# An attention-and-MLP kernel: later additions of narrow inputs, another bank, 1e-9 on VectorE and matmuls of 128 columns

## The chip, the cores and the metric

The kernel runs on one core of a Trainium2 chip. The metric is device time in microseconds (us), the median of some runs. The core has TensorE (PE in the profile; PEld is its loading of weights), VectorE (DVE), ScalarE (ACT), GpSimd (POOL) and SyncE (SP), which here starts all transfers between memories. Each engine takes its own instructions in order and waits on semaphores for the others.

## What is computed

Attention with a local causal softmax and a linear memory branch, gated per head, and behind it two MLPs in a row:

```python
scores = np.matmul(q, k.transpose(0, 1, 3, 2)) / sqrt(D)     # B, H, S, D = 4, 8, 576, 64; causal
a = exp(scores - max); a /= a.sum(-1) + 1e-09
local = a @ v
q_p = elu(q) + 1
mem_out = (q_p @ M_prev) / (q_p . z_prev + 1e-6)
x = g * mem_out + (1 - g) * local                             # g = sigmoid(beta), per head
x = elu(x.reshape(2304, 512) @ w_in) @ w_out                  # 512 -> 2048 -> 512
out = leaky(x @ w_in2, 0.01) @ w_out2
```

The weights of the MLPs come as 64-bit floats and are decoded on the chip.

## The kernel before

**Numbers as two parts.** Most matmuls work on fp32r, a 32-bit form whose products are less exact than fp32's. A number is kept as a high part (rounded to fp32r) and a low part (the rest), and a product is two or three matmuls. In batch 0 of attention the tensors are plain fp32 instead (`full_v`); the trace shows such a matmul as two records.

**Attention.** A `Pair` is two heads of one batch, 16 pairs in all; an `Item` is one head and one of two groups of queries (the first 256 tokens, the last 320), 64 in all. Tokens are cut into five chunks `CH`, of 128, 128, 64, 128 and 128. An item goes through three stages, woven so that item n is scored while item n-1 is transposed and item n-2 multiplied with v: `score` (matmuls of a chunk of queries with all earlier keys into a bank `sc`, of which there are three; DVE adds the mask and finds the extreme; ACT takes the exponential and its sum `ss`), `norm` (1e-9 is added to the sums on GpSimd, DVE takes the reciprocal `rs`, GpSimd scales the probabilities `pt`), `t0` to `t1c` (transposes into two `tp` banks, split into high `dh`, `ah` and low `dl`, `al` by ACT and DVE) and `pv` (the product with v and, in the same sum, of the memory branch's queries `qph`, `qpl` with M, into one bank `po`; batch 0 uses `pm`). `qp_unit` transposes those queries, in the same bank `po`, ahead of a pair's first `pv`. DVE copies the result to `xp` (L529), SP writes it to memory as `xq`, one tensor for each head of a pair and batch.

**Where half is zeros.** Chunk 0 has 128 keys, but its score matmul is made 256 wide (L414). The diagonal blocks of the probabilities stand in `dh`, `dl` or `d32` as four pieces of 128 columns; the first piece is zeros, set once, so that `vc[j, 1]` and `vc[j, 4]` can be multiplied with 256 columns, zeros and diagonal (L510, L518).

**The first MLP's first part, woven in.** `phase1_units(ti)` makes the work of one batch for seven of sixteen slices of 128 hidden numbers, as two parts of 288 tokens each. A part is `u_x` (SP loads x, as `xt` and, with the halves of the partitions exchanged, `x2`, tile `y`; DVE adds the two, four instructions, L684; ACT casts to `xh`, GpSimd takes the rest `xl`, and both go to memory), seven `u_h` (12 matmuls into `pm`, L616, then elu: ACT, ACT, DVE to `e`, L630, split into `gh` and `gl`) and four `u_o` (21 matmuls, L644). The tiles `x` and `y` exist once. Batch 0 is read from `xm` without an addition.

**What sets the order.** The loop over attention units emits this work as fill: from `DELAY` = 13000 (ns of planned PE work) behind the end of a batch, against a credit in proportion to the attention emitted, with a priority 20 instructions ahead. What is left goes into `side`, behind attention, together with the decoding of more weights. A scheduler then orders each engine's instructions by these priorities and a timing model of its own; the order that it made is what runs. Banks: `pm` 2, `sc` 3, `tp` 2, `po` 1.

Of the kernel before, what the change touches and what calls it, by code (L numbers as in the profile page):

```python
# [8 lines left out]
F32 = mybir.dt.float32  # L9
# [3 lines left out]
ALU = mybir.AluOpType  # L13
AX = mybir.AxisListType

P = 128
# [3 lines left out]
def _f(ap):  # L20
    return ap.bitcast(F32)
# [3 lines left out]
def kernel(  # L25
# [14 lines left out]
    nc = tc.nc  # L40
# [4 lines left out]
    NKC = DM // P  # L45
    NF = DFF // P
    NFA = 7
# [4 lines left out]
    V32 = 1  # L52
# [3 lines left out]
    HC = 1.0  # L56
    E_GH, E_WH, E_VH, E_MS, E_V32, E_XH, E_RS, E_Y = "V", "A", "V", "P", "P", "A", "P", "A"
    W2A, W2B = 1, 5
# [7 lines left out]
    EARLY = 150  # L66
    DELAY = 13000.0
    NHP = H // 2
    PSUM = bass.MemoryType.PSUM
# [134 lines left out]
    def bank(tag):  # L204
        return psum.tile([P, 512], F32, tag=tag, bufs=BANKS[tag], name=tag)
# [44 lines left out]
    class Pair:  # L250
# [69 lines left out]
        def qp_unit(self, grp):  # L320
            _, s0, n, cc = grp
            if grp is self.groups[0]:
                self.qph = at.tile([P, S], F32R, tag="qph", name="qph")
                self.qpl = at.tile([P, S], F32R, tag="qpl", name="qpl")
            tp = bank("po" if self.ti else "pm")
            for c in cc:
# [73 lines left out]
    class Item:  # L400
# [8 lines left out]
        def score(self, c):  # L409
# [3 lines left out]
            qs, kk, kl = pr.qs[j], pr.kk[0 if pr.full_v else j], pr.pad["kl", j]  # L413
            spans = [(0, nk, max(nk, 256))] if c < 4 else [(0, 288, 288), (288, 288, 288)]  # L414
            if c == 2:
# [82 lines left out]
        def pv(self):  # L498
# [8 lines left out]
            if gi == 0:  # L507
                for a in ("d32",) if full else ("dh", "dl"):
                    mms.append((0, n, pr.vc[j, 0], pd[a][:, 256:512]))
                    mms.append((0, n, pr.vc[j, 1], pd[a][:, 0:256]))  # L510
            else:
# [4 lines left out]
                for a in ("d32",) if full else ("dh", "dl"):  # L516
                    mms.append((64, n, pr.vc[j, 3], pd[a][:, 256:512]))
                    mms.append((64, n, pr.vc[j, 4], pd[a][:, 0:256]))  # L518
            if full:
# [138 lines left out]
    def phase1_units(ti):  # L658

        units = []  # L660
        for pi, (pt, o, w, _) in enumerate(parts):
            if pt != ti:
                continue
            st = {}

            def u_x(pi=pi, o=o, w=w, st=st):
                def split():
                    st["x"] = split_x(xt, w, pi % 2)
                    for n in range(2):
                        nc.sync.dma_start(xp_scr[n][pi], _f(st["x"][n]))  # L670
                    st["g"] = {}

                xt = mtile("x", 1, F32, (NKC, NW))[:, :, 0:w]
                if ti < V32:
                    nc.sync.dma_start(xt, xm_scr[ti][:, :, o:o + w])
                    split()
                    return
                x2 = mtile("y", 1, F32, (NKC, NW))[:, :, 0:w]
                for j in range(2):
                    ps, pz = slice(64 * j, 64 * j + 64), slice(64 - 64 * j, 128 - 64 * j)  # L680
                    nc.sync.dma_start(xt[ps], xq_scr[ti][j][ps, :, o:o + w])
                    nc.sync.dma_start(x2[ps], xq_scr[ti][j][pz, :, o:o + w])
                for c in range(NKC):
                    nc.vector.tensor_tensor(out=xt[:, c], in0=xt[:, c], in1=x2[:, c], op=ALU.add)  # L684
                split()

# [11 lines left out]

            units.append((0, u_x))
            for f in range(NFA):  # L700
                units.append((HC * 12 * w / 2.4, lambda f=f, u=u_h: u(f)))
            for ec in range(NKC):
                units.append((3 * NFA * w / 2.4, lambda ec=ec, u=u_o: u(ec)))
        return units

# [47 lines left out]
    for c, u, done in att:  # L753
# [7 lines left out]
        if done is not None:  # L761
            fill += [(pos + DELAY, c2, u2) for c2, u2 in phase1_units(done)]
        if fill and fill[0][0] <= pos:
# [164 lines left out]
```

## Time and profile before

| | us |
|---|---|
| median of 3 runs | 1096.52 (1096.45 to 1099.43) |
| the profiled execution | 1098.26 |
| its span, first to last instruction | 1096.2 |
| PE busy | 1057.6 |
| DVE busy | 600.3 |
| POOL busy | 530.6 |
| ACT busy | 484.8 |
| mean granted PE clock | 0.995 of full speed |

By the last P·V matmul of each batch, attention on batch 0 ends at 99.9 us, and batches 1, 2 and 3 end at 198.0, 306.2 and 404.1; the rest is MLP. Matmuls overlap and their ends are modelled, so a busy PE may still lose time between starts; how long a matmul holds PE is read from the distance of its start to the next start. Durations on POOL are rough. A wait is put down to the semaphore that came last by the profile.

### The profile page before, as it was taken

What the parts mean: (1) busy time and instruction counts of PE and PEld (TensorE: products, weight loads), DVE (VectorE), ACT (ScalarE), POOL (GpSimd) and SP (SyncE); (2) the same over time, 40 slices, a digit from 0 to 9 for tenths busy, and PEclk for the clock granted to TensorE, in tenths of its full rate; (3) what the DMA queues carried; (4) which work ended last, traced back from release to release, by engine and by line L of the source; (5) the groups of instructions that cost most, each with busy time, mean ns of one, the idle gap of its engine ahead of it and who ended that gap; (6) DMA issues with size and microseconds to landing.
All of it is one profiled execution on the core that took longest, in us unless ns stands there. A gap on an engine that the chain in (4) does not pass through costs nothing.

```text
span 1096.2 us, 17406 instructions
## 1 busy us (share of the span) xinstructions
PE 1057.6 (96%) x5904; PEld 912.7 (83%) x5904; DVE 600.3 (55%) x1398; ACT 484.8 (44%) x1169; POOL 530.6 (48%) x674
## 2 busy tenths in 40 slices
PE   6998899989998999999999999999999999999997
PEld 3777789979998999978877889888888888888896
DVE  6889987778878857566574314664321222232232
ACT  5988877777877645444343223432211110111110
POOL 7675675667667626455453224755422322222221
PEclk9999999999999999999999999999999999999999
DMA  7753643564365139665653304331200100010010
GB/s 181 189 144 91 188 115 99 124 169 145 78 178 156 59 81 271 225 215 185 219 189 119 98 18 116 135 116 39 77 1 1 58 20 1 1 39 1 1 39 20
DMA packets 151576, 115.05 MB, mean 105 GB/s; under 512 B 81728, under 2 KB 144192, under 8 KB 151488
## 3 DMA queue, kind: packets, MB, share of 16 engines
q1 hardware_dynamic: 151488, 113.95, 35.5%
q8 instruction: 47, 0.77, 0.3%
q14 instruction: 41, 0.34, 0.1%
HBM read 78.52 MB, written 31.85 MB: 101 GB/s over the span
## 4 chain that ended last, share of the span: by engine, by line
PE 73%; DMA 8%; DVE 7%; POOL 3%; ACT 3%; SPq 3%; issue 3%; DVEq 0%; POOLq 0%; ACTq 0%
PE pm L616 17%; PE sc L876 14%; PE tp L616 13%; PE sc L644 8%; PE po L876 4%; PE pm L644 4%; PE po L522 3%; PE tp L455 3%; PE po L644 2%; DMA wraw<-in_moe_w_out_dram 2%; DMA x<-xq 2%; SPq L212 2%; PE sc L426 1%; PE sc L427 1%; PE pm L522 1%
## 5 line engine op out<-in xcount | busy, mean ns | idle before, releaser
L623 POOL TENSOR_TENSOR gl<-e,gh 128x512 fp32r<-128x512 f32 (+2 forms) x181 | 199.8, 1108 | 369.8 <-DVE gh L241 291.9
L616 PE MATMUL tp<-xw,w 128*128 128x512 f32 (+1 forms) x504 | 145.4, 371 | 0.9 <-DVE e L630 0.9
L616 PE MATMUL pm<-xw,w 128*128 128x512 f32 (+1 forms) x496 | 143.9, 371 | 0.0
L876 PE MATMUL sc<-w,gh 128*128 128x512 f32 x448 | 137.7, 393 | 0.0
L449 POOL TENSOR_SCALAR pt<-pt,rs,omg 128x128 f32<-128x128 f32 (+4 forms) x160 | 102.7, 651 | 28.0 <-DVE rs L444 25.7
L616 PEld LDWEIGHTS tp<-xw,w 128*128 128x128 f32 x504 | 91.3, 188 | 19.7 <-DVE e L630 1.7
L644 PE MATMUL sc<-gh,w 128*128 128x512 f32 (+2 forms) x438 | 106.0, 343 | 1.1 <-DVE st L857 0.7
L616 PEld LDWEIGHTS pm<-xw,w 128*128 128x128 f32 x496 | 90.5, 188 | 18.5
L434 ACT ACTIVATE pt<-pt,mx 128x128 f32<-128x128 f32 (+4 forms) x160 | 93.2, 585 | 22.7 <-DVE mx L429 22.1
L876 PEld LDWEIGHTS sc<-w,gh 128*128 128x128 f32 x448 | 83.1, 188 | 17.9
L616 PE MATMUL tp<-xv,w 128*128 128x512 f32 (+1 forms) x252 | 93.2, 370 | 0.0
L616 PE MATMUL pm<-xv,w 128*128 128x512 f32 (+1 forms) x248 | 92.0, 371 | 0.0
L616 PE MATMUL pm<-xh,w 128*128 128x288 f32 x368 | 80.2, 305 | 9.1 <-DVE e L630 5.7
L635 ACT ACTIVATE e<-pm 128x512 f32<-128x512 f32 (+1 forms) x40 | 22.2, 556 | 150.3 <-PE pm L616 149.1
L455 PE MATMUL tp<-ident,pt 128*128 128x128 f32 x480 | 80.1, 276 | 8.0 <-DVE al L248 3.1
L241 DVE CAST gh<-e 128x512 fp32r<-128x512 f32 (+2 forms) x146 | 77.9, 537 | 16.9 <-PE po L644 4.2
L137 POOL TENSOR_TENSOR w<-wm,w 128x512 fp32r<-128x512 f32 x50 | 66.1, 1344 | 43.4 <-ACT w L239 43.4
L876 PE MATMUL sc<-w,gl 128*128 128x512 f32 x224 | 85.4, 393 | 0.0
L644 PEld LDWEIGHTS sc<-gh,w 128*128 128x128 f32 x438 | 74.6, 188 | 12.2 <-issue 1.5
L636 DVE TENSOR_TENSOR e<-tp,e 128x512 f32<-128x512 f32 (+1 forms) x40 | 25.5, 637 | 107.2 <-ACT e L635 107.1
L636 DVE TENSOR_TENSOR e<-pm,e 128x512 f32<-128x512 f32 (+1 forms) x40 | 25.5, 637 | 105.8 <-ACT e L635 105.8
L429 DVE CUSTOM_DVE_ANT_0 pt<-sc,mask 128x128 f32<-128x128 f32 (+4 forms) x160 | 69.4, 446 | 8.6 <-PE sc L427 4.3
(155 smaller groups left out, 2407.9 us busy)
## 6 DMA issues: line engine op xcount, KB each, us to landing
wraw<-in_moe_w_in_dram SPq DMA_DIRECT2D x32, 512.0 KB, 4.1
wraw<-in_moe_w_out_dram SPq DMA_DIRECT2D x32, 512.0 KB, 5.3
xh<-xh SPq DMA_DIRECT2D x8, 576.0 KB, 3.3
xl<-xl SPq DMA_DIRECT2D x8, 576.0 KB, 3.9
ys<-st SPq DMA_DIRECT2D x32, 144.0 KB, 3.0
x1s<-st SPq DMA_DIRECT2D x36, 128.0 KB, 1.9
x<-x1s SPq DMA_DIRECT2D x9, 512.0 KB, 3.9
out_dram<-st SPq DMA_DIRECT2D x36, 128.0 KB, 1.7
```

The costliest lines, as they stand in the source:

```text
L137: nc.gpsimd.tensor_tensor(out=w[:, 1, a], in0=t[:, a], in1=_f(w)[:, 0, a], op=ALU.subtract)
L241: (nc.vector if eng == "V" else nc.gpsimd).tensor_copy(dst, src)
L429: nc.vector.tensor_tensor_reduce(out=pt[0:m, k0:k0 + n], in0=sc[0:m, 0:n], in1=mk, op0=ALU.add, op1=ALU.min, scale=-0.125, scalar=mx[0:m, ...
L434: nc.scalar.activation(out=pt[0:m, 0:nk], in_=pt[0:m, 0:nk], func=AF.Exp, scale=-1.0, bias=mx[0:m, last:last + 1], accum_out=self.pd["ss"] ...
L449: nc.gpsimd.tensor_scalar(out=pt, in0=pt, scalar1=rs[0:m, i:i + 1], scalar2=omg[0:m, h:h + 1], op0=ALU.mult, op1=ALU.mult,)
L455: nc.tensor.transpose(dst, self.p[c][:, k0:k0 + kn], ident)
L522: nc.tensor.matmul(po[:, a:b], w, x, start=i == 0, stop=i == len(mms) - 1)
L616: nc.tensor.matmul(ph, wi[:, wj, kc, :], xx[:, kc, :], start=n_mm == 0, stop=n_mm == 11)
L623: nc.gpsimd.tensor_tensor(out=gl, in0=g, in1=_f(gh), op=ALU.subtract)
L636: nc.vector.tensor_tensor(out=t, in0=ph, in1=t, op=ALU.max)
L644: nc.tensor.matmul(py, wo[:, wj, ec * P:(ec + 1) * P], gg, start=opens and f == first and n_mm == 0, stop=closes and f == last and n_mm == 2,)
L876: nc.tensor.matmul(pos[tb], gg[:, tb * P:(tb + 1) * P], wo[:, wj, :], start=f == 0 and n_mm == 0, stop=f == NF - 1 and n_mm == 2,)
```

## The change

- `phase1_units` is cut anew. Loads of x become a unit of their own, `u_load`. Those of a batch's first part are emitted as soon as the batch is done; those of the second part after the first part's second `u_h`, and its additions and casts (`u_x`) after the sixth, where they stood ahead of its own first `u_h`. The fill of batches 1 to 3 starts `LATE` = 20000 behind the batch's end.
- `qp_unit` takes its bank from `sc` instead of `po`, except in batch 0.
- 1e-9 is added on DVE (`E_RS`).
- The score matmul of chunk 0 is 128 wide; the products with `vc[j, 1]` and `vc[j, 4]` are 128 wide, on the diagonal block alone.

```diff
-    E_GH, E_WH, E_VH, E_MS, E_V32, E_XH, E_RS, E_Y = "V", "A", "V", "P", "P", "A", "P", "A"
+    E_GH, E_WH, E_VH, E_MS, E_V32, E_XH, E_RS, E_Y = "V", "A", "V", "P", "P", "A", "V", "A"
+    LATE = 20000.0
...
-            tp = bank("po" if self.ti else "pm")
+            tp = bank("sc" if self.ti else "pm")
...
-            spans = [(0, nk, max(nk, 256))] if c < 4 else [(0, 288, 288), (288, 288, 288)]
+            spans = [(0, nk, nk)] if c < 4 else [(0, 288, 288), (288, 288, 288)]
...
-                    mms.append((0, n, pr.vc[j, 1], pd[a][:, 0:256]))
+                    mms.append((128, n, pr.vc[j, 1], pd[a][:, 128:256]))
...
-                    mms.append((64, n, pr.vc[j, 4], pd[a][:, 0:256]))
+                    mms.append((192, n, pr.vc[j, 4], pd[a][:, 128:256]))
...
+        mine = [(pi, o, w, {}) for pi, (pt, o, w, _) in enumerate(parts) if pt == ti]
+
+        def u_load(pi, o, w, st):
+            xt = st["t"] = mtile("x", 1, F32, (NKC, NW))[:, :, 0:w]
+            if ti < V32:
+                nc.sync.dma_start(xt, xm_scr[ti][:, :, o:o + w])
+                return
+            x2 = st["t2"] = mtile("y", 1, F32, (NKC, NW))[:, :, 0:w]
+            for j in range(2):
+                ps, pz = slice(64 * j, 64 * j + 64), slice(64 - 64 * j, 128 - 64 * j)
+                nc.sync.dma_start(xt[ps], xq_scr[ti][j][ps, :, o:o + w])
+                nc.sync.dma_start(x2[ps], xq_scr[ti][j][pz, :, o:o + w])
+
+        def u_x(pi, o, w, st):
+            xt = st["t"]
+            if ti >= V32:
                 for c in range(NKC):
-                    nc.vector.tensor_tensor(out=xt[:, c], in0=xt[:, c], in1=x2[:, c], op=ALU.add)
-                split()
+                    nc.vector.tensor_tensor(out=xt[:, c], in0=xt[:, c], in1=st["t2"][:, c], op=ALU.add)
+            st["x"] = split_x(xt, w, pi % 2)
...
+        units = [(0, lambda: u_x(*mine[0]))]
+        for k, (pi, o, w, st) in enumerate(mine):
...
             for f in range(NFA):
                 units.append((HC * 12 * w / 2.4, lambda f=f, u=u_h: u(f)))
+                if k + 1 < len(mine) and f == 1:
+                    units.append((0, lambda k=k: u_load(*mine[k + 1])))
+                if k + 1 < len(mine) and f == NFA - 2:
+                    units.append((0, lambda k=k: u_x(*mine[k + 1])))
...
-        return units
+        return lambda: u_load(*mine[0]), units
...
-            fill += [(pos + DELAY, c2, u2) for c2, u2 in phase1_units(done)]
+            fetch, more = phase1_units(done)
+            fetch()
+            start = pos + (DELAY if done < V32 else LATE)
+            fill += [(start, c2, u2) for c2, u2 in more]
```

The scheduler makes a new order from this on every engine. Three places follow. Lines of the changed kernel lie 1 higher in attention (L531 is L530 before) and up to 11 off in the MLP's first part.

SP's queue at the end of batch 1 (its tensors are `xq_0_86` and `xq_1_87`; `xq_0_88` and `xq_1_89` are batch 2's; `kk` copies serve the next pair's scores, `ys` is the first MLP's result). Before, well behind the last write of batch 1:

```order
L212 DMA qn<-in_q_dram 128x2x64 x2
L227 DMA zb<-in_z_prev_dram 128x256
L681 DMA x<-xq_1_87 64x4x288
L682 DMA y<-xq_1_87 64x4x288
L530 DMA xq_0_88<-xp 128x320
L697 DMA ys_109<-st 128x288
L682 DMA y<-xq_0_86 64x4x288
L530 DMA xq_1_89<-xp 128x256
L670 DMA xh_94<-xh_3624 128x1152
L682 DMA y<-xq_1_87 64x4x288
```

Now, with the last write of batch 1 in the first row:

```order
L531 DMA xq_1_87<-xp 128x320
L671 DMA x<-xq_1_87 64x4x288
L672 DMA y<-xq_1_87 64x4x288
L300 DMA kk_3160<-kk_3160 64x256
L213 DMA kn<-in_k_dram 128x3x64
```

and, 15 rows further on:

```order
L697 DMA ys_109<-st 128x288
L681 DMA xh_94<-xh_3774 128x1152
L681 DMA xl_102<-xl_3775 128x1152
L671 DMA x<-xq_0_86 64x4x288
L672 DMA y<-xq_0_86 64x4x288
L671 DMA x<-xq_1_87 64x4x288
L672 DMA y<-xq_1_87 64x4x288
```

Loads of the first part now follow the write directly; those of the second part stand together right behind the writes of the first part's `xh` and `xl`.

DVE at the additions of batch 1's second part. Before (`e` is elu of the first part's hidden numbers):

```order
L385 SCALAR_TENSOR_TENSOR ph_f<-qn,ph_e 128x640
L429 ISA pt_3821,mx<-sc,mask 128x448
L429 ISA mx 128x1
L684 TENSOR_TENSOR x<-x,y 128x288 x2
L630 SCALAR_TENSOR_TENSOR e<-e,pm 128x288
L429 ISA pt_3828,mx<-sc,mask 128x288
L429 ISA mx 128x1
L684 TENSOR_TENSOR x<-x,y 128x288 x2
L248 TENSOR_TENSOR al<-tp,ah 128x320
```

Now (L444 is the 1e-9, new on this engine):

```order
L444 TENSOR_SCALAR rs<-ss_156 128x2
L445 RECIPROCAL rs<-rs 128x2
L249 TENSOR_TENSOR qpl<-sc,qph 128x320
L430 ISA pt_182,mx<-sc,mask 64x320
L430 ISA mx 64x1
L430 ISA pt_3556,mx<-sc,mask 128x448
L430 ISA mx 128x1
L678 TENSOR_TENSOR x<-x,y 128x288 x3
L530 COPY xp<-po 128x320
```

The additions still stand among attention's work, but later behind the loads that feed them.

PE near the end of batch 3, where the keys `kn` of the last pair are transposed. Before:

```order
L644 MATMUL pm<-gh,w_649 128x288 x2
L644 MATMUL pm<-gl,w_649 128x288
L644 MATMUL pm<-gh,w_792 128x288
L522 MATMUL po<-qph,ms_179 128x256
L522 MATMUL po<-qpl,ms_179 128x256
L522 MATMUL po<-dh_136,vv 128x256 x2
L522 MATMUL po<-dl_138,vv 128x256 x2
L292 MATMUL sc<-ident,kn 128x128 x3
L426 MATMUL sc<-kk_5289,qs_5361 128x288
L427 MATMUL sc<-kl_0_162,qs_5361 128x288
L644 MATMUL pm<-gh,w_792 128x288
```

Now:

```order
L617 MATMUL pm<-xl_5990,w_792 128x288
L293 MATMUL sc<-ident,kn 128x128 x2
L523 MATMUL po<-qph,ms_164 128x256
L523 MATMUL po<-qpl,ms_164 128x256
L523 MATMUL po<-dh_152,vv 128x256
L523 MATMUL po<-dh_152,vv 128x128
L456 MATMUL tp<-ident,pt_167 128x128
L456 MATMUL tp<-ident,pt_5494 128x128
L456 MATMUL tp<-ident,pt_5501 128x128
L523 MATMUL po<-dl_154,vv 128x256
L523 MATMUL po<-dl_154,vv 128x128
L293 MATMUL sc<-ident,kn 128x128 x3
```

MLP matmuls (L644) stood among attention's here; now the first of these rows is the last of the MLP for 99 matmuls. The pairs of 256 and 128 columns on `dh` and `dl` were pairs of 256.

## Rows read from the trace of the kernel before

**Rows 1.** The page: busy time, share of the span and instructions of each engine.

```profile
PE 1057.6 (96%) x5904; PEld 912.7 (83%) x5904; DVE 600.3 (55%) x1398; ACT 484.8 (44%) x1169; POOL 530.6 (48%) x674
```

**Rows 2.** Stretches: their length, busy us of engines (instructions), granted clock, DMA share, GB/s.

```profile
core 0: us, PE busy (x) PEld busy (x) DVE busy (x) ACT busy (x) POOL busy (x), PEclk, DMA share, GB/s
0.00:99.90 99.90, 88.74 (x452) 67.04 (x453) 80.74 (x239) 80.89 (x222) 65.17 (x128) 1.00 0.60 157
99.90:198.00 98.10, 90.14 (x665) 84.45 (x664) 83.34 (x246) 77.58 (x228) 68.86 (x110) 1.00 0.47 129
198.00:306.20 108.20, 102.78 (x776) 100.27 (x775) 86.74 (x264) 82.21 (x233) 72.10 (x117) 0.98 0.51 131
306.20:404.10 97.90, 92.88 (x702) 90.55 (x701) 75.34 (x215) 66.88 (x186) 57.59 (x87) 0.98 0.42 116
```

**Rows 3.** PE's waits: waiting group, what ended the wait: us in total, times, longest.

```profile
PE pm L616 <- DVE e L630: 5.7, 3, 2.8
PE pm L616 <- ACT xh L239: 3.4, 2, 1.8
PE po L522 <- DVE xp L529: 1.9, 4, 1.1
PE po L522 <- DVE qpl L248: 0.7, 1, 0.7
```

**Rows 4.** SP's queue at the end of batch 1: start us, us, instruction, count.

```profile
199.72 0.32 SPq L530 DMA_DIRECT2D xq<-xp  x1
...
214.12 0.54 SPq L681 DMA_DIRECT2D x<-xq  x1
```

**Rows 5.** DVE in order of time, at batch 1's additions; in brackets idle before.

```profile
221.29 2.17 DVE L684 TENSOR_TENSOR x<-x,y 128x288 f32<-128x288 f32 x4 [4.79 <-issue]
...
243.25 0.83 DVE L684 TENSOR_TENSOR x<-x,y 128x288 f32<-128x288 f32 x2 [2.07 <-DMA x<-xq]
```

**Rows 6.** PE in order of time, at four places.

```profile
121.37 0.81 PE L616 MATMUL pm<-xh,w 128*128 128x288 f32 x4 [1.85 <-ACT xh L239]
...
222.27 0.53 PE L616 MATMUL pm<-xh,w 128*128 128x288 f32 x2 [1.52 <-ACT xh L239]
...
244.50 0.53 PE L616 MATMUL pm<-xh,w 128*128 128x288 f32 x2 [2.59 <-DVE e L630]
...
338.16 0.85 PE L616 MATMUL pm<-xh,w 128*128 128x288 f32 x2 [2.83 <-DVE e L630]
```

**Rows 7.** Stretches, columns as in rows 2: the granted clock is the third last number.

```profile
240.00:250.00 10.00, 7.41 (x44) 7.08 (x45) 7.93 (x24) 7.38 (x22) 8.02 (x12) 0.83 0.63 178
...
330.00:340.00 10.00, 7.17 (x49) 6.93 (x49) 7.04 (x18) 6.43 (x19) 5.67 (x9) 0.91 0.82 223
```

**Rows 8.** DMA issues: count, KB each, median us from issue to landing.

```profile
xq<-xp SPq DMA_DIRECT2D x24, 160.0 KB, 2.1
...
y<-xq SPq DMA_DIRECT2D x12, 288.0 KB, 4.6
```

**Rows 9.** One stretch, columns as in rows 2: attention without MLP work.

```profile
99.90:121.40 21.50, 16.91 (x113) 13.83 (x111) 20.64 (x63) 15.65 (x47) 15.25 (x26) 1.00 0.51 129
```

**Rows 10.** PE in order of time: plain fp32 (d, kk,q), fp32r (dh, dl), transposes (tp).

```profile
54.19 0.39 PE L424 MATMUL sc<-kk,q 128*128 128x128 f32 x2
...
55.18 1.03 PE L522 MATMUL pm<-d,vv 128*128 128x256 f32 x4
56.04 0.70 PE L424 MATMUL sc<-kk,q 128*128 128x320 f32 x2
...
208.27 0.40 PE L522 MATMUL po<-dh,vv 128*128 128x256 f32 x2
208.51 0.40 PE L522 MATMUL po<-dl,vv 128*128 128x256 f32 x2
...
213.54 0.82 PE L455 MATMUL tp<-ident,pt 128*128 128x128 f32 x6
```

**Rows 11.** Groups by line and form: count | busy us, mean ns | idle before.

```profile
L444 DVE RECIPROCAL rs<-rs 128x2 f32<-128x2 f32 x32 | 4.9, 152 | 2.4 <-POOL rs L443 2.3
...
L443 POOL TENSOR_SCALAR rs<-ss 128x3 f32<-128x3 f32 x32 | 7.5, 234 | 20.3 <-ACT pt L434 18.8
L443 POOL TENSOR_SCALAR rs<-ss 128x2 f32<-128x2 f32 x32 | 7.1, 223 | 13.2 <-ACT pt L434 11.1
```

More of the change, by code (lines that the diff above doesn't have):

```diff
@@ L658, in phase1_units @@
     def phase1_units(ti):
[L660 to L675, printed above, removed]
-                    split()
[L677 to L682, printed above, removed]
-                for c in range(NKC):
-                    nc.vector.tensor_tensor(out=xt[:, c], in0=xt[:, c], in1=x2[:, c], op=ALU.add)
-                split()
+        mine = [(pi, o, w, {}) for pi, (pt, o, w, _) in enumerate(parts) if pt == ti]
[12 more added lines that the diff above has]
+            if ti >= V32:
+                for c in range(NKC):
+                    nc.vector.tensor_tensor(out=xt[:, c], in0=xt[:, c], in1=st["t2"][:, c], op=ALU.add)
+            st["x"] = split_x(xt, w, pi % 2)
+            for n in range(2):
+                nc.sync.dma_start(xp_scr[n][pi], _f(st["x"][n]))
+            st["g"] = {}
+        units = [(0, lambda: u_x(*mine[0]))]
+        for k, (pi, o, w, st) in enumerate(mine):
             def u_h(f, w=w, st=st):
@@ L697, in u_o @@
                 nc.sync.dma_start(y_scr[pi][:, ec], y)
-            units.append((0, u_x))
             for f in range(NFA):
                 units.append((HC * 12 * w / 2.4, lambda f=f, u=u_h: u(f)))
+                if k + 1 < len(mine) and f == 1:
+                    units.append((0, lambda k=k: u_load(*mine[k + 1])))
+                if k + 1 < len(mine) and f == NFA - 2:
+                    units.append((0, lambda k=k: u_x(*mine[k + 1])))
             for ec in range(NKC):
                 units.append((3 * NFA * w / 2.4, lambda ec=ec, u=u_o: u(ec)))
-        return units
+        return lambda: u_load(*mine[0]), units
     def merge(a, bu):
```

## Prediction

> **What bounds the kernel now.** I read the busy shares first: TensorE (PE) is busy for 96% of the span, no other engine for more than 55% [rows 1]. A busy PE of overlapping matmuls can still hide lost time, so next I cut the span at the last P·V matmul of each batch of attention [rows 2]. In the first 99.9 us (batch 0, with weights being decoded) PE is busy 88.7, VectorE (DVE) 80.7, ScalarE (ACT) 80.9; in the next three stretches PE is busy 90.1 of 98.1, 102.8 of 108.2 and 92.9 of 97.9 us, DVE 83.3, 86.7 and 75.3. So PE is the bound and DVE stands close behind it while attention runs. Idle PE in the three stretches is 8.0 + 5.4 + 5.0 = 18.4 us: that is what better order can win there. After 404 us there is nothing but MLP matmuls, which the change leaves as they are.
>
> Then I read who ends PE's waits [rows 3]: DVE's e (5.7 us), ACT's xh (3.4), DVE's xp (1.9), DVE's qpl (0.7). The e waits look like slow activation work, but the real cause is one step back. In batch 1 the last write of xq goes out at 199.72 and the loads that read it at 214.12 [rows 4], 14.4 us later. DVE reaches the additions x+y at 216.5 and stands still for 4.79 us; at 243.25 it stands still for 2.07 us more, for the second half of the batch [rows 5]. DVE takes its instructions in order, so the elu results e queued behind these additions are late, and so is PE: 1.85 us idle at 121.37, 1.52 at 222.27 (xh itself), 2.59 at 244.50 and 2.83 at 338.16 (e behind the additions of a second half) [rows 6]. After the last two the granted clock is 0.83 over 240 to 250 us and 0.91 over 330 to 340 [rows 7]: at the lower of its two levels for a part, after the engine had stood; 1.7 and 0.9 us of work are missing by these rows.
>
> **The change part by part.** *Loads and additions of x.* Each batch is two parts of 288 tokens. Loads of the first part are now issued behind the batch's last write; loads of the second after the second of the first part's seven hidden units, and its additions after the sixth. In the new order the eight loads of batch 1 stand right behind what they need, and about 50 DVE instructions lie between the additions of one part and those of the next, 20 us at 108.2 us for 264 of them [rows 2]. The transfers take 4.6 us [rows 8], so the second parts of batches 1 and 2 find their input there: 2.59 + 2.83 idle and 1.7 + 0.9 of clock, 8.0 us. The first parts gain less: their additions stand only 16 DVE instructions (6.6 us) behind the copy that feeds the last write, and write plus load take 2.1 + 4.6 us and an issue of 0.5, 7.2 us [rows 4, 8]. DVE may still stand there for 0 to 2 us instead of 4.79. Of the 1.52 + 1.85 us I count 1.5. Together -9.5 (bounds -11.4 and 0). The early loads add a wait: on SyncE's queue, which starts all transfers in order, the load stands until the write has landed, 2.1 us, and behind it stand the kk copies of the next pair, for whose scores PE would wait. Those scores come an item later, so I count nothing; at worst it is 2.1 for each of three batches, +6.3.
>
> *What the moved order costs.* The fill of MLP work into attention starts 20 instead of 13 us of planned work after batches 1 and 2. By the order, 110 PE matmuls stood without MLP work after batch 0, now 40; in exchange there is a run of 99 near the end of batch 3, where 57 was the longest, and a run of 9.8 us across the boundary of batches 2 and 3. Attention alone is slow: from 99.9 to 121.4 PE's 110 matmuls, 13.7 us at the slots below, took 21.5 us with DVE busy 20.6 [rows 9]; 7.8 us were lost, 1.85 of them counted above. The runs over 2.5 us add up to 49 us before and after, so by that the exchange costs nothing; I take +2.5, because at the end of batch 3 less MLP work is left to hide a late DVE. Bounds: -3 and +10 (12.2 + 9.8 us of such PE work, losing 0.57 us for each, less 2.5).
>
> *Matmuls of 128 columns in place of 256, plain fp32.* 16 in batch 0's P·V, two records each in the trace. A record of 256 columns occupies PE for 0.215 us (four from 55.18 to 56.04), one of 128 for 0.11 (two take 0.39, of which the end is 0.28) [rows 10]. 32 x 0.105 = 3.4 us off PE; but in that stretch DVE and ACT are busy as much as 81% and PE isn't alone on the path, so I take half: -1.7 (bounds -3.4 and 0).
>
> *The same in fp32r.* 48 score matmuls and 96 P·V matmuls of batches 1 to 3: 144. At 256 columns one takes 0.12 us (208.27 to 208.51 are two) [rows 10]. No fp32r matmul under 256 columns is in this trace, so bounds from both sides. Below: time by columns alone, 0.06, which saves 144 x 0.06 = 8.6 us. Above: the same 128 columns as plain fp32, two records of 0.11, so 0.22: a loss of 144 x 0.10 = 14.4 us. The nearest rows are single records of 128 columns with a weight load of their own, transposes (six in 0.82 us) and halves of plain fp32, all at 0.11 [rows 10]. I take 0.11: -1.4. On this the Trainium skill speaks against the change: its page "TensorE: Matmul & The Clock Gate", section "LDWEIGHTS (loading the stationary operand)", has a load cost columns/1.2 ns, 107 for 128 columns, however few columns stream behind it; the 0.11 of these rows agrees. The same page's "Back-to-back issue gap" has pairs of load and matmul at 128 columns flow at 81 ns; by it the term would be -5.6 instead of -1.4 and the time 1082. No row here is that fast.
>
> *Queries of the memory branch in the scores' banks.* They leave the one po bank, which the P·V matmuls need; 24 groups of transposes now share three banks with the scores. The wait on qpl (0.7) goes, the wait on xp (1.9) stays [rows 3]: -0.7 (bounds -2.6, and +1 where a score waits for a bank).
>
> *1e-9 on DVE.* 64 instructions leave GpSimd (0.22 to 0.23 us each) and their hand-over to DVE goes; DVE gets 64 of about 0.15, the price of its reciprocal of the same shape [rows 11], so 9.8 us of work, against up to 6.4 us for which it stood before that reciprocal. Behind DVE's wait for the exponentials stand masks and splits that PE needs, but they stood behind the reciprocal's wait as well. 0 (bounds -3 and +3).
>
> Sum: -9.5 + 2.5 - 1.7 - 1.4 - 0.7 + 0 = -10.8. The profiled execution took 1098.26 us (span 1096.2), so 1087.5. It stood 1.74 above the median of the runs (1096.52), so I forecast 1085.7, in round numbers **1086**.
>
> **The rivals.** *Narrow fp32r matmuls cost what plain fp32 costs* (slower). Place: first score chunk and the two P·V diagonals of batches 1 to 3. Price 0.22 in place of 0.11: 15.8 us more than in my sum, 1102. It decides against the change from a slot of about 0.185 on (10.8 us more). For it: fp32r is told from fp32 in these rows at 256 columns and above only. Against: the load rhythm of 0.11 explains every 128-column row.
>
> *The attention-only runs eat the gain.* Upper bound of the order's cost, +10 + about 1 in place of 2.5: 1095, no change that counts. For it: DVE was busy 96% of the time in the one such run that the trace has. Against: there is no more of it in sum than before.
>
> *The additions still wait*, since their loads stand directly behind a write that has to land; then only the small terms remain, -3.8: 1093. Against: the 50 DVE instructions between the parts.
>
> *Narrow matmuls go by columns*: 7.2 us more gain, 1079.
>
> **How the numbers follow.** Forecast 0.52 (its own range 1079 to 1092, from -3 to 0 on the order and 0 to 5 on waits that stay), fp32r slot 0.20, attention-only runs 0.14, additions still wait 0.09, by columns 0.05. The range is 1077 to 1101: it leaves out about half of the slow-slot rival and the tail below the last one. A measurement of this kernel tells 0.3%, 3.3 us, from no change. Faster than 1093.2: all of the first and the last, half of the fourth, some of the third, 0.66. Within: the rest of the third and fourth and some of the second, where DVE's pace hides a part of the longer matmuls, 0.18. Slower than 1099.8: 0.16.
>
> **What would show it.** Fp32r score and P·V matmuls of 128 columns: next start after 0.11 (right), 0.22 (first rival) or 0.06. DVE's stand ahead of x+y: under 2 us in place of 4.79 at a first part, none in place of 2.07 at a second, and the clock there at 1.00. Plain fp32 records of 128 columns: 0.11. In the stretch of batch 3, idle PE should collect in one place near its end, of 4 to 7 us; over 12 would be the second rival. No wait of PE for qpl. What would make me wrong beyond these: a kk copy held behind the early loads on the queue that starts all transfers, seen as scores that wait for a DMA.

## The result, and the profile after

The changed kernel takes **1111.39 us** (1110.35 to 1112.25, 4 runs) where the kernel before takes 1096.49 (1094.52 to 1099.43, 4 runs): a ratio of 1.0133, 95% interval 1.0108 to 1.0158. It is 14.9 us slower; the forecast was 1086, 10.5 us faster, and the range ended at 1101.

First the busy shares of the changed kernel, which answer to [rows 1]:

```profile
PE 1063.3 (96%) x5904; PEld 917.6 (83%) x5904; DVE 612.8 (55%) x1462; ACT 485.8 (44%) x1169; POOL 515.4 (46%) x610
```

Nothing stands out: PE is busy 5.7 us longer, DVE has its 64 additions, GpSimd lost them. Next the four stretches, again cut at the last P·V matmul of each batch, as in [rows 2]; the granted clock is the third last number:

```profile
core 0: us, PE busy (x) PEld busy (x) DVE busy (x) ACT busy (x) POOL busy (x), PEclk, DMA share, GB/s
0.00:103.10 103.10, 89.53 (x457) 66.21 (x457) 85.49 (x258) 81.61 (x224) 61.47 (x111) 1.00 0.57 152
103.10:205.60 102.50, 96.38 (x728) 93.05 (x727) 88.24 (x262) 78.96 (x228) 67.67 (x98) 0.98 0.46 128
205.60:312.60 107.00, 101.28 (x767) 100.01 (x767) 87.33 (x263) 78.62 (x222) 64.01 (x89) 0.97 0.48 127
312.60:413.50 100.90, 89.29 (x609) 82.82 (x608) 77.71 (x235) 64.81 (x184) 53.05 (x74) 0.92 0.40 111
```

The last line is the one to read. Batch 3 takes 3.0 us more than before and has 93 matmuls less in it (609, not 702): the MLP work that filled it is still to be done when attention ends. With a price for each shape of matmul (the distance to the next start where nothing waits, as in [rows 10]) the PE work of batch 3 is 76.6 us, so 24.2 of its 100.9 us are lost; before, 8.6 of 97.9 were. Batch 0 loses 24.7 where it lost 18.4; batches 1 and 2 are as good as before or better (10.4 and 9.4, before 13.5 and 9.3). Together that is 18.9 us more lost; the slots of the narrow matmuls are 4.6 us less, and the span is 14.2 us longer. Two places carry it: 15.6 us in batch 3 and 6.3 in batch 0. Batch 3's clock is 0.92, where it was 0.98.

A good part of batch 3's loss lies in two runs of attention matmuls without MLP work between them, 78 and 99 long; the first begins 4.6 us ahead of batch 3:

```profile
307.96:323.86 15.90, 12.37 (x81) 10.60 (x79) 13.81 (x43) 11.15 (x34) 8.78 (x14) 0.89 0.69 171
376.69:396.36 19.67, 16.30 (x102) 13.56 (x100) 18.09 (x62) 13.96 (x42) 9.22 (x12) 0.91 0.16 45
```

DVE is busy 92% of the second one: as in [rows 9], attention alone goes at DVE's pace. At the slots these matmuls are 9.8 and 12.2 us of work, so 13.6 of the 35.6 us are lost. The kernel before loses time in such runs too. By the same slots, the runs of more than 2.5 us of attention work in batches 1 to 3 lose 16.3 us before (48.9 us of work) and 24.4 now (48.5): 8.1 more. All else in these batches loses 14.8 before and 19.5 now. PE's granted clock falls too, in these runs and behind the wait for the additions at 344.74 (below):

```profile
320.00:330.00 10.00, 8.49 (x50) 7.39 (x50) 8.01 (x21) 5.68 (x16) 5.86 (x9) 0.85 0.75 163
340.00:350.00 10.00, 7.49 (x51) 7.11 (x49) 7.01 (x18) 7.73 (x22) 4.98 (x8) 0.85 0.36 83
350.00:360.00 10.00, 9.05 (x50) 8.92 (x49) 7.77 (x21) 5.25 (x15) 7.93 (x11) 0.64 0.42 97
```

Over the whole span the mean clock is 0.987 where it was 0.995: 1110.4 x 0.013 = 14 us against 1096.2 x 0.005 = 5, so by this estimate at most 9 of the 15 us are missing by the clock (less where PE stood anyway); in the stretches above it is at its lower level (1.2 in place of 2.4 GHz) for a part, behind stands of PE.

The additions of x, which were to find their input there: DVE in order of time at the four places, as in [rows 5].

```profile
214.43 1.19 DVE L678 TENSOR_TENSOR x<-x,y 128x288 f32<-128x288 f32 x3 [1.44 <-DMA y<-xq]
...
236.93 1.20 DVE L678 TENSOR_TENSOR x<-x,y 128x288 f32<-128x288 f32 x3 [2.73 <-DMA y<-xq]
...
322.88 1.19 DVE L678 TENSOR_TENSOR x<-x,y 128x288 f32<-128x288 f32 x3 [1.74 <-DMA y<-xq]
...
344.74 2.16 DVE L678 TENSOR_TENSOR x<-x,y 128x288 f32<-128x288 f32 x4 [2.92 <-DMA y<-xq]
```

First parts stand 1.44 and 1.74 us where 0 to 2 was said, down from 4.79. The second parts, for which none was said, stand 2.73 and 2.92. Their four loads go out close together on SP's queue:

```profile
226.07 1.10 SPq L671 DMA_DIRECT2D x<-xq  x1
227.22 1.31 SPq L672 DMA_DIRECT2D y<-xq  x1
228.58 0.83 SPq L671 DMA_DIRECT2D x<-xq  x1
229.45 0.61 SPq L672 DMA_DIRECT2D y<-xq  x1
```

They start behind the writes of the first part's `xh` and `xl` (the tiles x and y exist once), 11.6 us after that part's additions began at 214.43, and the additions that wait for the last of them begin 7.5 us after 229.45, not 4.6 [rows 8]. PE's waits, the longest groups, against [rows 3]:

```profile
PE sc L427 <- DVE mx L430: 4.4, 3, 2.5
PE sc L293 <- DMA kn<-in_k_dram: 4.2, 1, 4.2
PE po L523 <- DVE xp L530: 3.9, 4, 1.7
PE pm L617 <- ACT xh L240: 3.8, 3, 1.9
...
PE pm L617 <- DVE e L631: 2.9, 2, 1.9
...
PE sc L427 <- DVE qpl L249: 1.6, 1, 1.6
```

The wait for e is halved (5.7 before), that for xh is not, that for xp has doubled (1.9), and new at the top are scores that wait for DVE's masks (mx). Two of these waits come from the additions of x. On DVE the copy to xp at 238.04 and a mask at 346.82 follow the second parts' additions, and PE stands until they are done:

```profile
238.58 0.39 PE L523 MATMUL po<-qph,ms 128*128 128x256 f32 x1 [1.73 <-DVE xp L530]
```

```profile
347.50 0.61 PE L427 MATMUL sc<-kk,qs 128*128 128x288 f32 x1 [2.51 <-DVE mx L430]
```

With these two, the waits for e and xh come to 10.9 us. The kernel before had one such wait, 1.05 us for xp at 223.85; counted in the same way it stood 10.2. So what PE loses behind the additions has other names now and is not less. And the wait for qpl has moved: P·V no longer waits for it, but a score does, 1.6 us where it was 0.7.

### The profile page after: what moved, and what is told of

Its sections match the earlier page's. It is cut to its first block, busy times and chain, and to the rows that moved or that the text cites. A ratio compares the mean times of both kernels' runs of the same rounds, so it can differ in the third digit from the quotient of the medians.

```text
span 1110.4 us, 17405 instructions
## 1 busy us (share of the span) xinstructions
PE 1063.3 (96%) x5904; PEld 917.6 (83%) x5904; DVE 612.8 (55%) x1462; ACT 485.8 (44%) x1169; POOL 515.4 (46%) x610
## 4 chain that ended last, share of the span: by engine, by line
PE 77%; DVE 8%; DMA 5%; ACT 4%; issue 2%; SPq 2%; POOL 1%; DVEq 0%; ACTq 0%; POOLq 0%
PE pm L617 17%; PE tp L617 14%; PE sc L882 14%; PE sc L645 8%; PE pm L645 4%; PE po L882 4%; PE po L523 3%; PE tp L456 3%; PE po L645 3%; DMA y<-xq 2%; DMA wraw<-in_moe_w_out_dram 2%; PE pm L523 2%; PE sc L427 1%; PE sc L428 1%; DVE pt L430 1%
## 5 line engine op out<-in xcount | busy, mean ns | idle before, releaser
L624 POOL TENSOR_TENSOR gl<-e,gh 128x512 fp32r<-128x512 f32 (+2 forms) x181 | 197.4, 1093 | 385.7 <-DVE gh L242 305.9
L450 POOL TENSOR_SCALAR pt<-pt,rs,omg 128x128 f32<-128x128 f32 (+4 forms) x160 | 100.1, 634 | 68.1 <-DVE rs L445 38.9
L645 PE MATMUL sc<-gh,w 128*128 128x512 f32 (+2 forms) x466 | 111.8, 341 | 3.0 <-DVE gh L242 3.0
L435 ACT ACTIVATE pt<-pt,mx 128x576 f32<-128x576 f32 (+4 forms) x160 | 93.2, 584 | 32.8 <-DVE mx L430 31.2
L456 PE MATMUL tp<-ident,pt 128*128 128x128 f32 x480 | 85.5, 284 | 5.3 <-ACT ah L246 2.3
L645 PEld LDWEIGHTS sc<-gh,w 128*128 128x128 f32 x466 | 79.2, 188 | 13.7 <-DVE gh L242 3.5
L617 PE MATMUL pm<-xh,w 128*128 128x288 f32 x368 | 82.5, 310 | 6.6 <-ACT xh L240 3.8
L636 ACT ACTIVATE e<-pm 128x512 f32<-128x512 f32 (+1 forms) x40 | 22.2, 555 | 150.0 <-PE pm L617 149.9
L242 DVE CAST gh<-e 128x512 fp32r<-128x512 f32 (+2 forms) x146 | 73.9, 509 | 20.4 <-PE po L645 7.5
L636 ACT ACTIVATE e<-tp 128x512 f32<-128x512 f32 (+1 forms) x40 | 22.1, 554 | 117.5 <-PE tp L617 117.5
```

The source lines that it names most:

```text
L242: (nc.vector if eng == "V" else nc.gpsimd).tensor_copy(dst, src)
L435: nc.scalar.activation(out=pt[0:m, 0:nk], in_=pt[0:m, 0:nk], func=AF.Exp, scale=-1.0, bias=mx[0:m, last:last + 1], accum_out=self.pd["ss"] ...
L450: nc.gpsimd.tensor_scalar(out=pt, in0=pt, scalar1=rs[0:m, i:i + 1], scalar2=omg[0:m, h:h + 1], op0=ALU.mult, op1=ALU.mult,)
L456: nc.tensor.transpose(dst, self.p[c][:, k0:k0 + kn], ident)
L617: nc.tensor.matmul(ph, wi[:, wj, kc, :], xx[:, kc, :], start=n_mm == 0, stop=n_mm == 11)
L624: nc.gpsimd.tensor_tensor(out=gl, in0=g, in1=_f(gh), op=ALU.subtract)
```

## The experiments

**Theories.** *Holes*: the thin fill of MLP work in batch 3, which the second rival priced at 10 us, is the loss. *Work*: one of the parts costs more than its rows said. *Order*: each edit lets the scheduler draw a new order on every engine, and the order of the kernel before is better than most draws.

### One part undone

Each starts from the changed kernel.

```diff
-            tp = bank("sc" if self.ti else "pm")        # e1
+            tp = bank("po" if self.ti else "pm")
-    E_RS = "V"                                          # e2 (in its line)
+    E_RS = "P"
-    LATE = 20000.0                                      # e3
+    LATE = 13000.0
```

e4 takes back the three lines of the narrow matmuls.

> The changed kernel with one part undone: the memory branch's queries are transposed into the po bank again. Theory H (holes): the 15 us come from stretches in which PE has only attention's matmuls, above all near the end of batch 3, where attention runs at DVE's pace and PE's clock falls. By the order, MLP work emitted among attention in batch 3 rises from 29.9 to 36.0 us here and the longest run without it falls from 12.2 to 5.8 us, so H expects about 1100 (1095 to 1104), batch 3 shorter by 6 to 12 us and the granted clock over 300 to 400 us above 0.95. Theory B (bank): the queries' transposes take scores' banks and PE's scores wait for them; B expects the same direction but by PE's waits on sc alone (8.5 us in the changed kernel, back to about 1), clock unchanged: about 1104. Theory R (1e-9 on DVE) and theory W (narrow matmuls): 1108 to 1113.

1107.31 us, ratio 1.0081 (1.0056 to 1.0106): 4.1 us better than the changed kernel, and over the ranges of H and B. In its trace (of its fastest execution, 1102.35) batch 3 is 6.1 us shorter and the clock over 300 to 400 us is 0.97, not 0.91, as H said; but batch 2 is 7.2 us longer. PE's scores wait 11.3 us for masks, where they waited 8.3, against B.

> The changed kernel with 1e-9 back on GpSimd. Theory R: DVE waits for the exponentials with masks and splits queued behind it, and has 64 more instructions; R expects 1099 to 1104 and batch 0 back from 103.1 to about 100 us. Theory H: by the order batch 3 keeps 29.9 us of MLP work and a run of 15.9 us without, so 1108 to 1114. B and W: 1108 to 1113.

1108.21 us, 1.0101 (1.0052 to 1.0150). Batch 0 ends at 96.0 us, so R's sign came, but not its time.

> The changed kernel with LATE = 13000, so that the fill starts as early as before. The 99-matmul run near the end of batch 3 is split (7.9 and 5.3 us), the run across the boundary of batches 2 and 3 is 6.1 in place of 9.8, MLP work in batch 3 stays 29.9 us. Theory H expects 1105 to 1109 (some 4 to 6 us of attention-only PE work less, 0.57 us and some clock for each). If the late start itself were the cause (theory L): 1098 to 1103. R, B, W: 1109 to 1113.

1105.56 us, 1.0073 (1.0050 to 1.0096), as H said.

> The changed kernel with all matmuls 256 wide again, plain fp32 ones too. If narrow fp32r matmuls cost a slot of 0.22 in some form that the trace hides (theory W): 1097 to 1101. If they are worth 0.01 us each and the plain fp32 ones 3.4 us in all, as the slots of the changed kernel's trace say: 1111 to 1115. H: by the order batch 3 keeps 29.9 us of MLP work and a run of 12.1, so no gain.

1113.07 us, 1.0144 (1.0112 to 1.0176), as the slots said.

No part, undone, brings back the time: e1 to e3 give 3 to 6 us each (4.5 to 7.2 by the distance to the kernel before, which took 1097.83 beside them), all in orders drawn anew; and e4 says that the narrow matmuls are not what slowed the kernel.

### One part alone

Each starts from the kernel before and takes one part of the change: the moved loads and additions with `LATE` (e5), the bank (e6), the additions of 1e-9 (e7), the narrow matmuls (e8).

> The kernel before with the loads and additions of x moved alone (with LATE = 20000). By the order, MLP work among attention is 42.6, 40.3 and 42.8 us in batches 1, 2 and 3 and no run without it is over 5.3 us after batch 0 (the kernel before: 33.5, 46.9, 43.8, and a run of 13.7). Theory H expects a gain from this: 1084 to 1092. The rival of the prediction that the additions still wait, because four loads of 288 KB at once land in 7 us and not in 4.6: 1090 to 1096. If the moved loads themselves hurt (kk copies behind them): above 1100.

1106.92 us, 1.0071 (1.0048 to 1.0094). Here H missed by 15 us. Without a long run the attention-only runs lose 15.9 us in batches 1 to 3, no more than before; all else there loses 19.6, where it lost 14.8.

> The kernel before with the memory branch's queries in the scores' banks alone. By the order, batch 2 has a run of 14.7 us of attention alone in place of batch 1's 13.7, MLP work is 44.7, 37.1 and 37.5 us in place of 33.5, 46.9 and 43.8. Theory H: 1096 to 1104, batch 2 the longer one. Theory B (waits for sc): 1102 to 1108 with PE's waits on sc at 6 us or more. If neither: 1093 to 1097.

1105.85 us, 1.0076 (1.0051 to 1.0102), in B's range; PE's scores wait 7.2 us for masks (2.4 before).

> The kernel before with 1e-9 on DVE alone. Theory R (it lengthens DVE's chain): 1101 to 1107, batch 0 at 103. My prediction's 0 (-3 to +3): 1093 to 1100. By the order it keeps a run of 12.6 us after batch 0; MLP work 38.0, 45.8, 40.4.

1112.05 us, 1.0125 (1.0092 to 1.0158), over both forecasts.

> The kernel before with the matmuls of 128 columns alone. By the slots of the changed kernel's trace (a narrow fp32r matmul starts its successor 0.06 us later, but the successor's own slot is longer by 0.05) the fp32r ones are worth 1.4 us and the plain fp32 ones 3.4 us at most: 1090 to 1096. Theory W: 1106 or more. By the order MLP work is 42.3, 38.3 and 45.1 us and no run is over 3.4 us in batch 3; theory H by itself: 1092 to 1098.

1103.74 us, 1.0048 (1.0026 to 1.0070), between the forecasts.

Each part alone is slower, by 5 to 14 us, and they don't add up: together they would be +36, and the change is +15. Even the narrow matmuls lose 5 us, though they take 4.6 us of slots off PE. That speaks for the order, and it makes free-order runs a poor measure of a part: each measures the part and a new order at once.

### Part and order, apart

So the next runs hold the order. The kernel is built twice; the first build gives the order of all engines, and the second gets it as edges, from each instruction to the next one on its engine:

```diff
+def pin(tc, ins, order):
+    info = mybir.DependencyInfo(mybir.DependencyClass.NoSync, mybir.DependencyReason.DATA)
...
+        if e in last:
+            tc.add_manual_dep(ins[k], ins[last[e]].name, info, reason="order of the first build")
+        last[e] = k
...
+    for NEW in (False, True):     # first build with the old part, second with the new; e10, e12: (True, False)
```

The bank and the moved loads were not tried in this way; for them no run tells the part from the order.

> The kernel before with the 128-column matmuls alone, and with every engine's instructions held in exactly the order that the kernel before has (the order is read off a first build with 256 columns, and the second build gets it as edges from each instruction to the next one on its engine). Theory of the order (each edit lets the scheduler draw a new order on all engines, and a drawn order other than the one of before costs 5 to 15 us by itself): with the order held, only the 4.6 us of TensorE slots that the narrow matmuls save are left, so 1092 to 1096 us. Theory of the work (the narrow matmuls themselves cost more than their slots show, in the slot behind them or in the clock): 1101 to 1106 us, as in the run of the narrow matmuls with a free order (1103.7).

1098.54 us, 1.0009 (0.9990 to 1.0028): no change, between the two forecasts.

> The kernel before, all matmuls at their old 256 columns, but every engine's instructions in the order that the scheduler drew for the 128-column matmuls (the order of the run of the narrow matmuls alone). No instruction differs from the kernel before, only the order. Theory of the order: 1104 to 1109 us, the 1103.7 us of the narrow run plus up to the 4.6 us of slots given back. Theory of the work: 1096 to 1099 us, the time of before.

1104.15 us, 1.0062 (1.0041 to 1.0083): not one instruction differs from the kernel before, and it is 7 us slower.

> The kernel before with the 64 additions of 1e-9 on VectorE, and all other instructions of all engines held in the order of before. Theory of the order: 1095 to 1099 us, no change. Theory of the work (the addition queued on VectorE behind other work delays the reciprocal, the scaling and so the transposes): 1105 to 1113 us, as with a free order (1112.05).

1109.48 us, 1.0106 (1.0079 to 1.0133): the order is that of before, and it is 12 us slower.

> The kernel before with the 64 additions of 1e-9 on GpSimd as before, and all other instructions of all engines in the order that the scheduler drew when they were on VectorE. Theory of the order: 1105 to 1113 us. Theory of the work: 1096 to 1099 us, the time of before.

1116.95 us, 1.0172 (1.0142 to 1.0201): again the instructions of the kernel before, and 20 us slower, over the range of the order's theory.

| | order of before | order drawn for the part |
|---|---|---|
| 256 columns | 1097.06 | 1104.15 |
| 128 columns | 1098.54 | 1103.74 |
| 1e-9 on GpSimd | 1097.06 | 1116.95 |
| 1e-9 on VectorE | 1109.48 | 1112.05 |

1103.74 and 1112.05 are e8 and e7, beside which the kernel before took 1098.00. Two causes come apart. The narrow matmuls neither cost nor gain in either order; the 5 us of e8 were the order's. The 1e-9 on VectorE costs 12 us in the order of before, so there the theory of the order fell. (In the drawn order it gains 5 against GpSimd; that order was drawn with the additions on VectorE.)

Where the 12 us come from is in e11's rows. Below, the groups of the additions on DVE in e11 and in the changed kernel, then a group of the kernel before; the three numbers behind the count are the shortest, the median and the longest duration in ns:

```profile
L444 DVE TENSOR_SCALAR rs<-ss x64: 132/174/5682, 11.8 to 400.1; 128x2 f32<-128x2 f32 x32, 128x3 f32<-128x3 f32 x32
```

```profile
L444 DVE TENSOR_SCALAR rs<-ss x64: 127/169/2254, 12.1 to 399.3; 128x2 f32<-128x2 f32 x32, 128x3 f32<-128x3 f32 x32
```

```profile
L391 DVE SCALAR_TENSOR_TENSOR den<-den,ging x16: 149/170/3753, 20.1 to 378.8; 128x10 f32<-128x10 f32 x16
```

The median is the 0.15 to 0.17 us that the prediction took from the reciprocal. But one addition of two numbers in a partition took 5.68 us, 28 of the 64 took over 0.3, and all that is over 0.18 adds up to 23.9 us. Here is the longest one in e11, DVE and then GpSimd, in order of time:

```profile
140.32 0.48 DVE L530 COPY xp<-po 128x320 f32<-128x320 f32 x1
140.72 5.68 DVE L444 TENSOR_SCALAR rs<-ss 128x2 f32<-128x2 f32 x1
146.32 0.61 DVE L430 CUSTOM_DVE_ANT_0 pt<-sc,mask 128x448 f32<-128x448 f32 x1
```

```profile
139.95 1.57 POOL L388 TENSOR_TENSOR ph_e<-ph_f,zb 128x640 f32<-128x640 f32 x1
141.47 0.33 POOL L375 TENSOR_TENSOR ms<-mr,ms 64x64 fp32r<-64x64 f32 x1
141.75 3.12 POOL L610 TENSOR_TENSOR xl<-x,xh 128x288 fp32r<-128x288 f32 x4
144.81 1.57 POOL L624 TENSOR_TENSOR gl<-e,gh 128x288 fp32r<-128x288 f32 x2
```

```profile
146.99 0.39 PE L427 MATMUL sc<-kk,qs 128*128 128x256 f32 x1 [1.73 <-DVE mx L430]
```

GpSimd works through eight instructions without a gap from 139.95 to 146.38, and the addition on DVE ends 0.03 us behind the last. Behind it stand masks, and behind these PE. Of the 28 long ones, 23 end in the same way, within 0.03 us of the end of a GpSimd instruction, and five 0.22 to 0.26 us behind one. The Trainium skill has a rule for this on its page "SBUF — State Buffer", section "SBUF: two separate sides": VectorE and GpSimd share one pair of ports to SBUF, an exclusive lock that an instruction of either holds whole; on VectorE it is taken by instructions in a two-port mode, or with two inputs in SBUF against a GpSimd instruction that reads SBUF. The page "VectorE: DVE Perf Modes" of the Trainium skill, section "What auto-detection actually checks", has the two-port mode taken where firmware enables it for the instruction, one source and the destination lie in SBUF and their outer dimensions are both even or equal; the additions have such operands. The rows agree: 5.68 us beside GpSimd's eight instructions, where the median is 0.17. They add that VectorE did not get its turn between these eight. The row of L391 shows that the kernel before had it in sight: 0.17 us in the median, 3.75 once.

Is it the form of the instruction, or the place in DVE's queue? With every queue held, e13 and e14 swap the addition for a RECIPROCAL of the same tile and size (these two, e15 and e17 leave the 1e-9 out, so they price it and do not compute the same):

```diff
-            nc.vector.tensor_scalar(out=rs, in0=ss, scalar1=1e-9, scalar2=None, op0=ALU.add)
-            nc.vector.reciprocal(rs, rs)
+            nc.vector.reciprocal(rs, ss)
+            nc.vector.reciprocal(rs, ss)
```

> The run with 1e-9 on VectorE in the order of before (1109.48 us), every queue the same, but in the place of each addition stands a RECIPROCAL of the same tile and size, and the second RECIPROCAL reads the sums as well; the 1e-9 is left out. Theory of the lock (the addition's TENSOR_SCALAR form waits until GpSimd's elementwise instructions end, the RECIPROCAL form does not): the stretched time falls away (23.9 us of VectorE), 1096 to 1100 us. Theory of the place (the first instruction on the sums waits for ScalarE at the head of VectorE's queue, whatever its form): 1107 to 1111 us, as before the swap.

1100.76 us, 1.0014 (0.9996 to 1.0033): no longer told from the kernel before, and 0.8 over the lock's range. Its group of the swapped instructions:

```profile
L445 DVE RECIPROCAL rs<-ss x64: 128/165/178, 11.7 to 386.6; 128x2 f32<-128x2 f32 x32, 128x3 f32<-128x3 f32 x32
```

The same place in the queue, never over 0.178 us: it is the form, held up by GpSimd.

> The changed kernel, all engines held in its own order, with the same swap: a RECIPROCAL in the place of each addition of 1e-9, the 1e-9 left out. In the changed kernel 17 of the 64 additions are stretched, by 10.2 us in all. Theory of the lock: 1102 to 1108 us, since about half of what the swap gave back in the order of before is at stake. Theory of the place: 1110 to 1113 us, no change.

1112.14 us, 1.0122 (1.0098 to 1.0146). Here the theory of the lock missed: in the changed kernel's own order taking the stretching away gives nothing back. In the trace attention ends 2.6 us earlier (410.8, not 413.5; batch 0 at 100.2, not 103.1), but the MLP behind it takes 2.5 us longer. Batch 3 still loses 23.1 us, so something else sets the time there.

### The hole closed

e15 combines the narrow matmuls, in the order of before, with a reciprocal that reads the sums itself. e16 takes the changed kernel with the bank of e1 and spreads the fill (`RESERVE` is the planned MLP work, in ns, that the fill leaves for behind attention), in an order drawn anew; e17 holds e16's order and drops the additions.

```diff
-    RESERVE = 60000.0
+    RESERVE = 50000.0
```

> The kernel before in its own order, with the 128-column matmuls, and with the 1e-9 left out: the RECIPROCAL reads the sums itself, and GpSimd has 64 additions of 0.23 us less. If the narrow matmuls' saving of 4.6 us of slots was eaten by waits for the scaled scores: 1090 to 1095 us. If it goes in the granted clock, whatever the waits: 1096 to 1099 us.

1095.90 us, 0.9981 (0.9964 to 0.9999): 2 us better than before, which the prediction's 3.3 us count as no change, and at the edge between the two forecasts.

> The changed kernel with the queries' transposes back in the bank po (run e1: 1107.3 us) and with the constant RESERVE at 50000 in place of 60000, which spreads the first MLP's matmuls further: 39.6 us of them stand among the attention of batch 3 (36.0 in e1, 29.9 in the changed kernel, 43.8 in the kernel before) and no run of attention matmuls there is longer than 4.7 us. Theory of the holes (the thin fill of batch 3 carries most of the loss): 1098 to 1103 us, with a batch 3 whose loss is 9 to 11 us. Theory of the order and the lock (the additions on VectorE and the drawn order carry it): 1104 to 1111 us, wherever the holes lie.

1100.41 us, 1.0023 (1.0008 to 1.0039): 6.9 us under e1, 11 under the changed kernel. The time is in the range of the theory of the holes, but the sign that it named did not come: batch 3 loses 16.4 us, not 9 to 11, and e1's batch 3 lost 15.1 already. Over batches 1 to 3 the attention-only runs lose 10.4 us, where the changed kernel's lose 24.4; all else there loses 22.2, where it was 19.5. So the holes account for a good part against the changed kernel, as far as a run with another bank and a new order can say.

> The run e16 (queries' transposes in the bank po, RESERVE 50000; 1100.4 us), all engines held in its own order, with the 1e-9 left out: the RECIPROCAL reads the sums itself, and the 64 additions with their 15.8 us of stretching fall away from VectorE. If the stretched additions are on the path once the hole is closed, as in the order of before: 1092 to 1097 us, under the kernel before. If they are beside the path, as in the changed kernel's own order: 1099 to 1102 us.

**1093.88 us, 0.9955 (0.9932 to 0.9978): faster than both kernels**, without the 1e-9. In e16's order the additions cost 6.5 us. Batch 3 of e16 and of e17:

```profile
308.90:408.60 99.70, 90.61 (x656) 87.12 (x656) 77.64 (x222) 62.40 (x176) 55.59 (x75) 0.95 0.40 112
```

```profile
303.80:402.40 98.60, 90.99 (x656) 87.05 (x656) 73.06 (x210) 62.53 (x176) 55.15 (x75) 0.95 0.42 114
```

Against the changed kernel 47 of the 93 missing matmuls are back, the loss of batch 3 falls from 24.2 to 16.4 and 15.3 us, and the clock rises from 0.92 to 0.95.

## Why the prediction was wrong

The steps in their order.

**Loads and additions, -9.5: the gain did not come.** DVE's stand at first parts shrank as said (4.79 to 1.44). At second parts it did not vanish (2.73 and 2.92), since the step priced a load at the 4.6 us of the median and did not ask what four loads of 288 KB cost that go out together, behind the first part's writes: 7.5 us from the last issue. PE's waits for e and xh went from 9.1 to 6.7 us, where 6.9 of them were to go, and the waits for xp and a mask behind the same additions, 1.73 and 2.51, take that back (10.9 in all, 10.2 before). The 2.6 us of clock did not come either: PE's clock is lower than before. On this step the third rival, at 0.09, was right.

**The moved order, +2.5: too small.** By the rows above, the attention-only runs lose 8.1 us more, near the bound of +10. The run of 99 matmuls and the run over the boundary were in the text, and the bound was worked out from 0.57 us lost for each us of such work; the two runs lost 13.6 of 35.6 us, 0.62 for each of 22.0. The working was right and the choice wrong: "the runs over 2.5 us add up to 49 us before and after" set long runs equal to short ones, but in these two PE falls to DVE's pace and for a part to the lower clock. e16, without such long runs, loses 14.0 us less in them than the changed kernel; e5 has none either and is 9 us slower than before, so they are not the whole cause. The rival "attention-only runs eat the gain" had the mechanism; it started from a gain that wasn't there.

**Order in general: missing.** The prediction costed each part in the order of before, or by what stood at single places of the new one. e10 changes nothing but the order and costs 7 us; e8 is that order again. e12 does the same with another order and costs 20. No term stood for it.

**1e-9 on VectorE, 0 (-3 to +3): wrong by its mechanism.** It took the duration from the reciprocal, a form that GpSimd does not hold up. In the order of before the term is +12.4 (e11), of which the form is 9 to 10 (e13); in a better-filled version of the change it is +6.5 (e16 to e17). In the changed kernel itself the same swap gave nothing in sum (e14): batch 0 ends 2.9 us earlier with it, and as much is lost again behind attention. So what the 1e-9 adds to the 14.9 us depends on what else is late; e2's 3.2 us came with a new order. Why the gain is lost in that one order stays open, and so does the rest of batch 0's loss.

**Plain fp32 at 128 columns, -1.7: right in its slot.** Records of 128 columns take 0.11. What they are worth in time no run shows by itself.

**Fp32r at 128 columns, -1.4: right in its slot, and no rival came true.** The changed kernel's P·V of 256 and 128 columns, and the next group:

```profile
209.45 0.34 PE L523 MATMUL po<-dh,vv 128*128 128x256 f32 x2
209.63 0.39 PE L523 MATMUL po<-dl,vv 128*128 128x256 f32 x2
209.86 0.51 PE L293 MATMUL sc<-ident,kn 128*128 128x128 f32 x3
```

The four take 0.41 us where they took 0.48 [rows 10], which looks like the rival by columns. But the start behind a narrow one comes after 0.06 and the next only after 0.17: what is won at one start is given back at the next. In e9, where the order is that of before, 48 such groups win 0.064 us by the fourth start and 0.02 by the fifth and later ones, 0.01 for each narrow matmul: a slot of 0.11 as said. The 107 ns that the Trainium skill gives for a weight load, on its page "TensorE: Matmul & The Clock Gate", section "LDWEIGHTS (loading the stationary operand)", agree with this 0.11; the 81 ns of that page's "Back-to-back issue gap" are not seen in these groups. Yet in e9 none of the 4.6 us arrived: the mean clock of its runs is 0.991 where the 20 runs of before beside it have 0.994, 3 us of the span. Whether the narrow matmuls themselves lower it was not tried.

**The bank, -0.7: wrong in sign.** Back in `po` the kernel is 4.1 us faster (e1), alone it costs 8 (e6), both in free orders; the wait for qpl went from P·V to a score and grew (0.7 to 1.6), that for xp doubled, and scores wait for masks. How much of it is the bank and how much the order stays open.

**The ends.** From the changed kernel, e1, e16 and e17 lead to 1093.9 us: -4.1 for the bank, -6.9 for the fill, -6.5 for the additions, each given the ones ahead of it, the first two in orders drawn anew. What remains there, loads, additions of x and narrow matmuls with a fill spread again, is 4.2 us under the kernel before (1098.03 in that comparison), not 10.8; and a part of the 4.2 can be the 1e-9 left out, which in the order of before was worth some 3 us (e9 to e15). So the cause of the 14.9 us is known in part: where they are lost is read from the rows, the price of the 1e-9 and that of an order are shown with the order held, and how the holes, the bank and the order share the rest stays open.

## What to carry to other kernels

Where a scheduler orders the program, an edit's largest cost can be the new order: hold the old one by edges to see what the edit itself is worth, and run the new order without the edit to see the rest. Before an instruction moves to VectorE, read the longest duration of its form, not the median, and look at what GpSimd runs beside it. A run in which one kind of work stands without its filler is priced by its length: two runs of 78 and 99 matmuls lost 0.62 us for each us of their work.

## What the runs showed of the hardware

A TENSOR_SCALAR of two numbers in a partition on VectorE took up to 5.68 us beside GpSimd's elementwise work, while a RECIPROCAL of the same tiles at the same place never took over 0.178. Behind a 128-column fp32r matmul the next start comes after 0.06 us and the one behind it after 0.17, 0.23 for two, as long as two records of 128 columns with a weight load each take (0.11). And 7 us lie between two kernels whose instructions are all the same and only stand in another order.
